# A TensorE-bound kernel: three reads of x in half-height tiles, and block products that put the second half's wide matmuls ahead of the first half's narrow ones

## The chip, the cores and the metric

One NeuronCore of a Trainium2 chip runs the kernel. The metric is device time in microseconds of one execution. Five engines work beside one another and wait for one another through semaphores: TensorE (PE; its weight loads are listed as PEld), VectorE (DVE), ScalarE (ACT), GpSimd (POOL) and SyncE (SP), which issues the DMAs.

## The reference

```python
def _attn_ref(x, state):                       # x 8,8,512,64   state 8,8,32,64
    scores = scale * np.matmul(x, state.transpose(0, 1, 3, 2))
    a = softmax(scores)                        # with 1e-9 added to the sum
    xread = np.matmul(a, state)
    scores2 = scale * np.matmul(state, x.transpose(0, 1, 3, 2))
    a2 = softmax(scores2)
    sread = np.matmul(a2, x)
    return np.concatenate([xread, sread], axis=2)

def reference(...):                            # 8*544 rows of 512
    x = attn_out.transpose(0, 2, 1, 3).reshape(B * S, H * D)
    g = softplus(x @ w_in)                     # 512 x 2048
    return g @ w_out                           # 2048 x 512
```

All is float32. "softmax" stands here for subtracting the maximum, exp, and dividing by the sum plus 1e-9.

## The kernel before, in words

The batches 0 to 7 each have 512 rows of x; the 32 state rows of all eight batches form a ninth block of 256 rows, called batch 8. Every kind of work is a generator, and every generator has a letter. The string PLAN (L40) is 1758 letters long; the loop at L977 takes it letter by letter and runs the next step of that generator. All instructions are kept in that order on their engine, so PLAN is the order of each engine's queue. For steps that several engines can do, ENG (L58) holds one letter a step: D for DVE, A for ACT, P for POOL. On-chip buffers are named rooms (L107), handed out first in, first out: eight PSUM banks (tiles named b), and in SBUF the classes s (12), d (17), g (8) and v (4).

The steps that matter here, by their letters:

- v (v_product) and Q (scores) call heads (L347): eight float32 matmuls of 64 rows by 32 columns of the array, in eight places of it, 512 columns each. The trace shows each as two matmuls.
- R (s_read, L541) multiplies the turned softmax a2T with x, one batch a step: for two values e, four chunks c and four column places q one float32 matmul of 128 rows by 32 columns with 64 columns moving, so 32 a step, 64 in the trace. The four chunks add up in one PSUM bank. r (s_scale, L557) multiplies the bank by the reciprocal sums on DVE and gives it back.
- t and y are transposes on TensorE, g (gemm1) is the first layer in groups of six 512-column matmuls, s is softplus on ACT.
- M (form_product, L868) is the second layer for batches 1 to 8. It is a block product with seven products in place of eight (the "forms" 1 to 7); each form of a team (a batch alone, the last team batches 8 and 7 together) is summed over two halves c = 0, 1. For each half, first come the "high" matmuls of 512 columns, then the "low" ones of 256 columns: 8 and 8 for a single batch, 12 and 12 for the last team. Then the half's operands are given back: Ahi and Alo (the split left operand) and Bt, the half's slab of weights, 1 MB in a g room. There are 49 forms, so 98 halves, in the order of UNITS2 (L796); the last half takes three M steps.
- J (slab_load, L800) fetches the slab of the next half from HBM into a g room. F, H and L (form_sum, form_hi, form_lo) prepare the left operand; k (chain) adds a finished product from its bank to the running sums; q (fold) and P (fold_store) finish and store them.

The functions that the change touches, with what calls them:

Of the kernel before, what the change touches and what calls it, by code (L numbers as in the profile page):

```python
# [15 lines left out]
ALU = mybir.AluOpType  # L16
# [3 lines left out]
P = 128  # L20
B, H, S, NS, D = 8, 8, 512, 32, 64
# [7 lines left out]
FAST = 1  # L29
F1, F2 = 4, 2  # L30
PIN = True


TURNS = [(0, 0, 16), (1, 0, 16)]
# [3 lines left out]
FORMS = (1, 2, 6, 5, 7, 3, 4)  # L38
# [8 lines left out]
    "q98MMtytvuhzHkkuLHlFFLZLhvRMMJJPJJMMHl9kHkhHLHhkLgMMlkirqkLqLklkkPTJJPPJJPJJXXvQvgse1fhshhlq1ell2qh3qggggsssfs"  # L47
    "4ggMgggsH2l53LgMg4ssssssgggssHs5Fk6ki7LFHFFHLFHFLtytMMMMkLH6uzkuLZqkHvvRJJJJPTMMhhLlHH7hlHh8q98FLLllkkrMMJJJTJ"
    "XPLFqHLqkk9HLMMgggMMsHsskkqkkkLkJPPJJPTJJXPvQv1khhql2qlee13ggggssshsHfhf42llLgggMgggsHFqL35sss4ssgggMsssH56F6k"
    "LFHkLFH7MMttyF8HqFLu7L9kuzHkLFMJPJPJJMMMJJPPJPPRvHZkkHFqLiLkHh8vMMkLlrHhHhHqLlLlkkH9LLqMJXPTJPPJJJJMgMggMssshk"  # L50
    "kHkklkkvvQge1hfsgggshsshH2Lll3h1l2leLFgggg4sssfsggggssssgMMM3FHFqsH4F5FqqLH5Lqk6LTPPJJJPMtytMMJJXJHFFHkLiuk7kH"
    "HHHzL6HLqLZkukLMMkFMvvRJJPh8hH7kLqlq9LrqLh8MMMJTJPXJJJPPXJPl9kHkhkkklgMMskklkvQvgghqHl1ehe2sfhfLlh13lqgggssss4"
    "Lq253qgggwiMyPssgHs45MgJzlsgFPLstkuJgkxsgssgtgsMH6sqL7H86PuMFZRLvvkrFJkhlvhlPvhhFFJHFLhlh97MHLlHHMHLMwFkMkHJJ8"
    "hLJJJlPq9MHgLkxsgkgMFsslPwgHgLJqPkLghkMqMgxkHsskgPkskgLJgJgsllqsPLMHLHyzMqZsPwssMkgggqLggskg&P&wsxsxMgkqwkx%%s"
    "wgswx&xqP&%s%s&g%w&wP%wJsxxgwJxxw&x%&%sF&gFw&wx%&%qxg%wHx&s&Lg%H%&sL%&&%s%sHLHLMFHMHFPFJFHHkJFLFLFLLFJkHMLMFJk"
    "JHLHFkkJMHHLHkLqMHkPLHkFLLJLJHMHLqLJHFkMHPFqkLJLHHkHPFLHMMLJkLMHLHkkkkLJMLqMkPkkHHqPqkqLkqLqPPqMPMkPqMPkqkPP"
)
ENG = {  # L58
    '&': "DDAADDADDDDADADA",
    '3': "PPDDDPPDPDDPDDDP",  # L60
    '6': "PPDPPPPDDPDDDPPP",
    '8': "PPDPAPDPDPPDAADPDD",
    '9': "DPDPDDDPPDPDDPDDPP",
    'B': "DAAADDAA",
    'D': "PDPAAADA",
    'E': "DDDPDPPD",
    'F': "DPDDDDDDPDPDPDDPDDPDPDDPDDPDPPDPPDPDPDDDPDPPDPPDDPDDDDPDDDDDDPDD",
    'H': "PAAAAPAAAADPAADAPAAAAAAPADPPAAPDDPPDAAPAADDAPDAADADDPAADAAAPAPAPAAPADAAAPAPAAAAPADADAADAAAAAAAAPAAAAPAAADAAAAPAA",
    'L': "DDDDDDDDPDPDPPPDDDDPPDDDPDPPPDPDDDPDDPPPPPDDPDDDPDDPDPDDDPDDDPDDDPDDDDPDPDPDDPPDPPPPPPDDDDDDDDDDPDPDPDDDPDDDDPDD",
    'U': "PPDDDPDP",  # L70
    'W': "AAADAPAD",
    'Y': "DDDPPPDD",
    'b': "AAAAADDDDD",
    'h': "AAAADADDDDDDDADAADADDDAADDAAADADAADDAADADAAAADAAAAADADADADADDAAAAAAA",
    'k': "AADDDDDDDDDDDDDDAADDDDDDDDDDDDDDAADDDDDDDDDDDDDDAADDDDDDDDDDDDDDDDDDDDDDDDDDDDDDAADDDDDDDDDDDDDDAADDDDDDDDDDDDDDDDDDDDDD",
    'm': "DAADAADAAAPADP",
    'n': "DDDPDDDPPDPDDD",
    'o': "AAAD",
    'q': "PPDPDPDDPDPDDPDPPPDDDDPPPPPPPDDPDDPPDDDPPPDDPDDDDPPPDPDPDDDD",
    'u': "DAADDAADDADADDDD",  # L80
    'w': "PADDADAAAAAAAAAA",
    'x': "DDPPPPDPDDDDDPDP",
    'z': "DDADAADA",
}


# [48 lines left out]
def attention_then_softplus_mlp(ctx: ExitStack, tc, xn, xt, zq, zp, stk, w_in, w_out, out):  # L135
    nc = Ordered(tc) if PIN else tc.nc
    TABLE = {AF.Softplus: "softplus", AF.Exp: "natural_log_exp_and_others", AF.Prelu: "natural_log_exp_and_others"}
# [14 lines left out]
    banks = Rooms(ps, "b", 8, [P, 512])  # L152
# [33 lines left out]
    xT, x, win, wraw = {}, {}, {}, {}  # L186
# [80 lines left out]
    up, low = {}, {}  # L267
# [122 lines left out]
    sc, T, e2, a2, pr, sr, aT = {}, {}, {}, {}, {}, {}, {}  # L390
# [21 lines left out]
    def rs(b, e):  # L412
        return few[b][:, 66 + e:67 + e]
# [118 lines left out]
    a2T = {}  # L532
# [7 lines left out]

    def s_read():  # L541
        for b in range(B):
            pr[b] = banks.take()
            for e in range(2):
                for c in range(4):
                    for q in range(4):
                        h = 2 * q + e
                        nc.tensor.matmul(pr[b][32 * q:32 * q + 32, D * e:D * e + D],
                                         a2T[b, e][:, P * c + 32 * q:P * c + 32 * q + 32],
                                         x[b, h // 4][:, c, D * (h % 4):D * (h % 4) + D], start=(c == 0), stop=(c == 3),  # L550
                                         tile_position=(0, 32 * q))
                a2T[b, e].done()
            x[b, 0].done()
            x[b, 1].done()
            yield

    def s_scale():  # L557
        for b in range(B):
            sr[b] = r1.take()
            nc.vector.tensor_tensor(sr[b].t.rearrange("p (e d) -> p e d", e=2), pr[b][:, 0:P].rearrange("p (e d) -> p e d", e=2),  # L560
                                    few[b][:, 66:68].unsqueeze(2).broadcast_to([P, 2, D]), ALU.mult)
            pr[b].done()
            few[b].done()
            yield

# [300 lines left out]
    prod = {}  # L866

    def form_product():  # L868
        for team, f, c in UNITS2:
            w = Bt[team[0], f, c]  # L870
            pairs = [(b, p) for b in team for p in range(1 if b == B else 2)]
            if c == 0:
                for k in pairs:
                    prod[k, f] = banks.take(uses=READS[f])
            def high(k, b, p):
# [7 lines left out]
            def low(k, b, p):  # L883
                nc.tensor.matmul(prod[(b, p), f][:, 0:256], Alo[b, f, c][:, k, P * p:P * p + P], w[:, k, 0],
                                 start=False, stop=(c == 1 and k == 3))

            if (team, f, c) == UNITS2[-1]:
                for n, pair in enumerate(pairs):
                    for of in (high, low):
                        for k in range(4):  # L890
                            of(k, *pair)
                    if n < 2:
                        yield
            else:
                for k in range(4):
                    for pair in pairs:
                        high(k, *pair)
# [50 lines left out]
    def fold_store():  # L948
# [90 lines left out]
```

## Time and profile before

| | us |
|---|---|
| median of 3 runs | 614.88 (614.83 to 615.35) |
| the profiled execution | 614.1 |
| its span, first to last instruction | 612.3 |
| PE busy | 597.5 (98%) |
| DVE, ACT, POOL busy | 477.1, 306.9, 303.9 |

The profile is of one execution on the one core. Busy time of PE is modelled at its ends and overlaps from one matmul to the next, so what a matmul costs is read from the distance of one start to the next and not from its duration. All operations bear line 100, a helper that records them, so rows are told apart by tiles and shapes.

### The profile page before, as it was taken

The numbers are of one execution on the slowest core, as the hardware profiler recorded it, in microseconds if no ns is written. First come the engines' busy times: TensorE is split into PE (matmuls) and PEld (weight loads), VectorE is DVE, ScalarE is ACT, GpSimd is POOL, SyncE is SP. The second block draws the span as 40 slices with busy tenths as digits, with TensorE's granted clock in tenths as the row PEclk, the third lists the DMA queues.
The fourth block names the chain that finished last, engine by engine and source line by source line (L and its number), as shares of the span: only waits on it lengthen the run. The fifth ranks groups of instructions, "written<-read, shape, count | busy, mean of one in ns | idle before, by whom it ended". The sixth has DMA issues, their size and how long they took to land.

```text
span 612.3 us, 10423 instructions
## 1 busy us (share of the span) xinstructions
PE 597.5 (98%) x4048; PEld 485.0 (79%) x4048; DVE 477.1 (78%) x644; ACT 306.9 (50%) x445; POOL 303.9 (50%) x190
## 2 busy tenths in 40 slices
PE   3999999999999999999999999999999999999997
PEld 1568677888788888878788787888787888888886
DVE  4999998799636896798479966699747944389996
ACT  4999767962526218631283318802675232274321
POOL 2422637517563761777276532672085955251561
PEclk9999999999999999999999999999999999999999
DMA  8999959999637888089917992699543851166572
GB/s 310 408 391 364 351 198 343 365 403 414 247 140 276 310 324 336 1 318 394 341 65 258 344 316 123 208 390 411 206 152 147 337 203 70 29 243 233 210 300 77
DMA packets 50415, 161.62 MB, mean 264 GB/s; under 512 B 4288, under 2 KB 29376, under 8 KB 37824
## 3 DMA queue, kind: packets, MB, share of 16 engines
q1 hardware_dynamic: 50368, 160.97, 70.5%
q8 instruction: 32, 0.52, 0.3%
q14 instruction: 15, 0.12, 0.1%
HBM read 137.36 MB, written 23.59 MB: 263 GB/s over the span
## 4 chain that ended last, share of the span: by engine, by line
PE 97%; DVE 1%; ACT 1%; DMA 1%; issue 0%; POOL 0%; SPq 0%
PE b L100 97%; ACT s L100 1%; DMA ST<-in_zp_dram 1%; DVE v L100 0%; DVE s L100 0%; POOL s L100 0%; SPq L100 0%; DVE W L100 0%; ACT ST L100 0%
## 5 line engine op out<-in xcount | busy, mean ns | idle before, releaser
L100 PE MATMUL b<-g,d 128*128 128x256 f32 (+1 forms) x1576 | 290.3, 337 | 0.0
L100 PEld LDWEIGHTS b<-g,d 128*128 128x128 f32 x1576 | 246.6, 190 | 36.1 <-issue 1.7
L100 PE MATMUL b<-d,d 128*128 128x512 f32 x744 | 177.2, 392 | 0.0
L100 PEld LDWEIGHTS b<-d,d 128*128 128x128 f32 x744 | 137.8, 188 | 32.3 <-issue 3.0
L100 ACT ACTIVATE g<-b 128x512 f32<-128x512 f32 x112 | 63.6, 600 | 98.7 <-PE b L100 98.3
L100 POOL TENSOR_TENSOR d<-g,d 128x1024 fp32r<-128x1024 f32 x31 | 78.6, 2538 | 53.0 <-ACT d L100 26.6
L100 DVE TENSOR_TENSOR s<-s,b 128x512 f32<-128x512 f32 (+1 forms) x105 | 68.7, 675 | 40.3 <-PE b L100 32.6
L100 DVE TENSOR_TENSOR d<-g,d 128x1024 fp32r<-128x1024 f32 x53 | 80.0, 1516 | 1.7 <-ACT d L100 1.5
L100 PE MATMUL b<-g,s 128*128 128x512 f32 (+1 forms) x280 | 71.4, 372 | 0.0
L100 ACT CAST d<-g 128x1024 fp32r<-128x1024 f32 x50 | 51.7, 1051 | 29.7 <-POOL g L100 15.8
L100 ACT ACT_TABLE_LOAD x48 | 61.6, 1283 | 1.5 <-PEq L1020 0.7
L100 PEld LDWEIGHTS b<-g,s 128*128 128x128 f32 x280 | 50.2, 188 | 12.0 <-issue 2.2
L100 ACT CAST d<-b 128x512 fp32r<-128x512 f32 x35 | 20.1, 586 | 59.3 <-PE b L100 59.3
L100 DVE TENSOR_TENSOR d<-b,d 128x512 fp32r<-128x512 f32 x62 | 41.4, 681 | 9.3 <-ACT d L100 9.0
L100 POOL TENSOR_SCALAR d<-g 128x1024 fp32r<-128x1024 f32 x20 | 29.5, 1476 | 36.2 <-DVE g L100 26.5
L100 POOL TENSOR_TENSOR s<-s,v 128x512 f32<-128x512 f32 x17 | 21.0, 1237 | 44.5 <-DVE v L100 43.9
L100 POOL TENSOR_TENSOR s<-s 128x256 f32<-128x256 f32 x29 | 29.9, 1032 | 21.1 <-DVE s L100 21.1
L100 POOL TENSOR_TENSOR d<-d,d 128x256 f32<-128x256 f32 (+2 forms) x17 | 28.3, 1664 | 18.6 <-DVE d L100 8.5
L100 PE MATMUL b<-W,ST 64*32 64x512 f32 (+2 forms) x544 | 32.6, 574 | 4.1 <-DVE W L100 4.1
L100 DVE TENSOR_REDUCE v<-s 128x16 f32<-128x512 f32 x32 | 21.6, 680 | 18.6 <-ACT s L100 18.5
L100 POOL TENSOR_TENSOR g<-g,g 128x1024 f32<-128x1024 f32 x11 | 29.4, 2671 | 11.2 <-DVE d L100 6.3
L100 ACT COPY s<-b 128x512 f32<-128x512 f32 (+2 forms) x32 | 15.2, 501 | 29.1 <-PE b L100 25.1
(82 smaller groups left out, 626.9 us busy)
## 6 DMA issues: line engine op xcount, KB each, us to landing
g<-slabs SPq DMA_DIRECT2D x98, 1024.0 KB, 6.6
d<-in_xt_dram SPq DMA_DIRECT2D x16, 512.0 KB, 7.4
g<-in_w_out_dram SPq DMA_DIRECT2D x8, 1024.0 KB, 12.5
d<-in_xn_dram SPq DMA_DIRECT2D x16, 512.0 KB, 7.6
slabs<-d SPq DMA_DIRECT2D x16, 512.0 KB, 6.9
out_dram<-s SPq DMA_DIRECT2D x56, 128.0 KB, 5.3
g<-in_w_in_dram SPq DMA_DIRECT2D x6, 1024.0 KB, 13.0
slabs<-g SPq DMA_DIRECT2D x24, 256.0 KB, 7.1
```

Of the source, the lines that this page charges most:

```text
L100: return lambda *a, **k: self.tc.keep_in_program_order(f(*a, **k))
```

## The change

Three things are changed.

SPLIT gives each batch a number of row halves for its read. For batches 4, 5 and 6 it is 2: each matmul of 128 rows becomes two of 64 rows, in the upper and the lower half of the array, which add up in two PSUM banks; s_scale then scales the first and adds the second with one scalar_tensor_tensor on DVE for each e. The other batches read as before.

JOIN has one letter for each of the 49 forms. At 20 of them it is J: the step of the half c = 0 issues its high matmuls alone and ends; the step of c = 1 issues its own high matmuls, then the low ones of half 0, gives the operands of half 0 back, then the low ones of half 1, and gives those back. The 29 others run as before. The forms with J are five of batch 2, six of batch 3, four of batch 4, four of batch 5 and one (form 7) of the last team.

PLAN is the same in its first 702 letters and in its last 53 and in another order between, with the same count of every letter. ENG changes for some of the steps.

```diff
+SPLIT = (1, 1, 1, 1, 2, 2, 2, 1)
+JOIN = ("--------JJJJJ-JJJJJJ-J-JJ--J-JJ-JJ------------J--")
...
     def s_read():
         for b in range(B):
-            pr[b] = banks.take()
+            halves = SPLIT[b]
+            pr[b] = [banks.take() for _ in range(halves)]
+            n = P // halves
             for e in range(2):
                 for c in range(4):
                     for q in range(4):
-                        h = 2 * q + e
-                        nc.tensor.matmul(pr[b][32 * q:32 * q + 32, D * e:D * e + D],
-                                         a2T[b, e][:, P * c + 32 * q:P * c + 32 * q + 32],
-                                         x[b, h // 4][:, c, D * (h % 4):D * (h % 4) + D], start=(c == 0), stop=(c == 3),
-                                         tile_position=(0, 32 * q))
+                        for o in range(halves):
+                            h, r = 2 * q + e, slice(n * o, n * o + n)
+                            nc.tensor.matmul(pr[b][o][32 * q:32 * q + 32, D * e:D * e + D],
+                                             a2T[b, e][r, P * c + 32 * q:P * c + 32 * q + 32],
+                                             x[b, h // 4][r, c, D * (h % 4):D * (h % 4) + D], start=(c == 0), stop=(c == 3),
+                                             tile_position=(n * o, 32 * q))
...
+            if SPLIT[b] == 2:
+                for e in range(2):
+                    t = sr[b][:, D * e:D * e + D]
+                    nc.vector.scalar_tensor_tensor(t, pr[b][1][:, D * e:D * e + D], rs(b, e), t, ALU.mult, ALU.add)
...
     def form_product():
+        held = []
         for team, f, c in UNITS2:
...
+            for k in range(4):
+                for pair in pairs:
+                    high(k, *pair)
+            held.append(c)
+            if c == 0 and JOIN[len(FORMS) * TEAMS.index(team) + FORMS.index(f)] == "J":
+                yield
+                continue
+            for d in held:
                 for pair in pairs:
                     for k in range(4):
-                        low(k, *pair)
-            for b in team:
-                Ahi[b, f, c].done()
-                Alo[b, f, c].done()
-            w.done()
+                        low(k, *pair, d)
+                finished(d)
+            held.clear()
             yield
```

The order of the TensorE steps around the reads of batches 4 to 7 goes from `vvR`, `Rvv`, `vvR`, `Rvvvv` to `Rvv`, `vvR`, `Rvv`, `Rvvvv` (each with M steps on both sides).

## Rows read from the trace of the kernel before

**Rows 1.** The page: span, busy time of the engine with most, granted clock by slice.
```profile
span 612.3 us, 10423 instructions
...
PE 597.5 (98%) x4048; PEld 485.0 (79%) x4048; DVE 477.1 (78%) x644; ACT 306.9 (50%) x445; POOL 303.9 (50%) x190
...
PEclk9999999999999999999999999999999999999999
```

**Rows 2.** The chain that ended last, shares by engine.
```profile
PE 97%; DVE 1%; ACT 1%; DMA 1%; issue 0%; POOL 0%; SPq 0%
```

**Rows 3.** The same chain in order of time: start us, us, what.
```profile
18.40 590.13 PE b L100 x3956
```

**Rows 4.** Waits of PE, longest and shortest of four: waiter, awaited, us in total, times, longest.
```profile
PE b L100 <- DMA ST<-in_zp_dram: 5.1, 1, 5.1
...
PE b L100 <- ACT s L100: 0.7, 1, 0.7
```

**Rows 5.** Timeline of PE: start, us, instructions; a read beside two or four heads calls.
```profile
342.15 1.10 PE L100 MATMUL b<-d,s 128*32 128x64 f32 x64
343.18 1.95 PE L100 MATMUL b<-W,ST 64*32 64x512 f32 x32
345.06 3.30 PE L100 MATMUL b<-g,d 128*128 128x512 f32 x17
...
413.07 1.95 PE L100 MATMUL b<-W,ST 64*32 64x512 f32 x32
414.95 1.10 PE L100 MATMUL b<-d,s 128*32 128x64 f32 x64
415.98 8.29 PE L100 MATMUL b<-g,d 128*128 128x512 f32 x45
...
468.15 3.66 PE L100 MATMUL b<-W,ST 64*32 64x512 f32 x64
471.75 2.11 PE L100 MATMUL b<-g,d 128*128 128x512 f32 x8
```

**Rows 6.** Busy time in the stretch of the first weight loads.
```profile
5.04:5.19 0.15, 0.09 (x8) 0.12 (x16) 0.00 (x0) 0.00 (x0) 0.00 (x0) 1.00 0.90 294
```

**Rows 7.** Timeline of PE, narrow stretches: where blocks of high and low matmuls start.
```profile
188.50 0.39 PE L100 MATMUL b<-g,d 128*128 128x512 f32 x1
190.31 0.52 PE L100 MATMUL b<-g,d 128*128 128x256 f32 x3
191.26 0.63 PE L100 MATMUL b<-g,d 128*128 128x512 f32 x2
193.10 0.52 PE L100 MATMUL b<-g,d 128*128 128x256 f32 x3
194.06 0.63 PE L100 MATMUL b<-g,d 128*128 128x512 f32 x2
```

**Rows 8.** A slab load's issue, the unit it feeds, landing times in 190 to 204.
```profile
191.46 0.33 SPq L100 DMA_DIRECT2D g<-slabs  x1
...
199.64 0.63 PE L100 MATMUL b<-g,d 128*128 128x512 f32 x2
...
DMA to landing us min/median/max: 4.7/4.8/5.0
```

**Rows 9.** Groups of DVE by shape: busy us, mean ns.
```profile
L100 DVE TENSOR_TENSOR d<-g,d 128x1024 fp32r<-128x1024 f32 x53 | 80.0, 1516 | 1.7 <-ACT d L100 1.5
L100 DVE TENSOR_TENSOR g<-g,g 128x1024 f32<-128x1024 f32 x17 | 23.0, 1356 | 0.4 <-ACT g L100 0.4
...
L100 DVE TENSOR_TENSOR v<-b,v 128x128 f32<-128x128 f32 x8 | 2.3, 282 | 2.6 <-PE b L100 2.5
```

**Rows 10.** Busy time of PE, PEld, DVE, ACT, POOL before and in the last team.
```profile
480.00:545.00 65.00, 65.00 (x345) 55.95 (x344) 35.76 (x58) 21.08 (x43) 33.38 (x20) 1.00 0.42 159
545.00:612.30 67.30, 63.51 (x373) 56.16 (x371) 57.30 (x73) 22.66 (x36) 27.91 (x18) 1.00 0.59 213
```

More of the change, by code (lines that the diff above doesn't have):

```diff
@@ L46 @@
     "gggsLkssss4vvMMgh5qkhlkHhdhsqLLqlllgMgggggMsssssFq67HkLJJJPJPPPXggggMssssHF8LHsHFM6LF7FHFLLkkHMMJJJPJHHkkqqkLL"
[L47 to L55, printed above, removed]
@@ L56 @@
-    "JHLHFkkJMHHLHkLqMHkPLHkFLLJLJHMHLqLJHFkMHPFqkLJLHHkHPFLHMMLJkLMHLHkkkkLJMLqMkPkkHHqPqkqLkqLqPPqMPMkPqMPkqkPP"
+    "q98MMtytvuhzHkkuLHlFFLZLhvRMMJJPJJMMHl9kHkLLgihhPqJJMHkkkgsTlMPkTHQrvklXsPvJhkXlh1LghXl23gJls1Jeqsg2ghsqs4fqg3"
+    "sg5MyFHsg4LgeLglf56gssgggssPgsMssFsFFHHqJkFLMPMHLtFH7HkJuJLtkMMH6J8LuRivHrkkvLqhhJMkPMJFHJlM9TL7PHklkJLFLzMZ8L"
+    "kPMH9hkMgHMkqsLkJqhLllgkgMTkHkQk1svHsvgseghglgsq2f3hgJlX41hsLLg2sHL3gle5sP4hlgs5sJqggqgFg6sssgs678sPsFMJMMkFfq"
+    "HHPHJkFLFMJt7qqLkykMLtHF9HJ8uJLMkPLHuJXPPMMvHh9JkzhJvkRkLLZJFlMMlhgPJkHgJHqLJsFMirLhHgJHlkMskLLPkMPMkTTskkqQHl"
@@ new lines @@
+    "vkJe1vgshgeX2hlhqshXgPlJgJgsTLsHqggss1l32fLlHgsgggsqgMsssLFPsHgFMs4LHMJFyfFPJt5LFiutqzJMMuk3HHFkq4J5HFPLM6LJM7"
+    "HLJqqMkRkJL6HkvHkHqk8Lrkv7hhqHllZMM9FhL8kJJkP9LlhMMgLHJksMkLMkvJPkkvHhlQkyhLlPgg1sz2gHPJsswggqhlhJ1LsJsPPegPXs"
+    "H23Zqefqf4LFMglMlgg53sgqisgsgPskg4sgP5skss6gq6JHMLtxtsFHquwPMHFkuFRvPJ7rLvFLh8hkvHlvlJMJFhlHhHLMlkhL9J7H8l9MMg"
+    "gkshFskHghsJkPqLMJFgsgsLgHMlLlJhJMsgHgqgssLkHsLPgkgMlksLJqPkygMgkkxPgqMwxsPkzHwqgsZHsksgg&%JwxxgwxLs&P%gqswxw&"
+    "wPM%&xLsJ&x%gw%&s&%&M%kwsx%gswxwxF&FgwxHqk&xg%&&w%Jsx&%&%wsx%gJH&%%LLJs&J%sFFFHHLMHFHHLFPFLFMLLMkFHFHLFMkJHHkk"
@@ L57 @@
+    "JqHHLLMLkHLPHMkLFLJLHMJqLJkkHHFLLJqMPHLqHkkJPFLPkHHFLJHHMMLJkLMHLHkkkkLJMLqMkPkkHHqPqkqLkqLqPPqMPMkPqMPkqkPP"
 )
 ENG = {
[L59 to L63, printed above, removed]
+    '&': "AAAADAAAAADDADDA",
+    '3': "PPDDDPPDPDPDDDPP",
+    '6': "PPDPPPPDDDPDDPDD",
+    '8': "PPDPAPDPDPPADAAPAA",
+    '9': "DPDPDDDPPDDPPPDDPD",
     'B': "DAAADDAA",
@@ L66 @@
     'E': "DDDPDPPD",
-    'F': "DPDDDDDDPDPDPDDPDDPDPDDPDDPDPPDPPDPDPDDDPDPPDPPDDPDDDDPDDDDDDPDD",
-    'H': "PAAAAPAAAADPAADAPAAAAAAPADPPAAPDDPPDAAPAADDAPDAADADDPAADAAAPAPAPAAPADAAAPAPAAAAPADADAADAAAAAAAAPAAAAPAAADAAAAPAA",
-    'L': "DDDDDDDDPDPDPPPDDDDPPDDDPDPPPDPDDDPDDPPPPPDDPDDDPDDPDPDDDPDDDPDDDPDDDDPDPDPDDPPDPPPPPPDDDDDDDDDDPDPDPDDDPDDDDPDD",
+    'F': "DPDDDDDDPDPDPDDPDDPDPPPPDDDPDDDDDDPDPDPDDDPPDPPPDDDDDDDDDDDDPDDD",
+    'H': "PAAAAPAAAADPAADAPAAAAAAPADPDAAAPAADAAAAPDADAAPDDDPDPDPPAPDDDADAPAAPDDAPDPAAAPPPDDPDPPAAAPAAAAAAADDAPAADDAAPAAPAA",
+    'L': "DDDDDDDDPDPDPPPDDDDPPDDDDPPPPDPDDDPPDPPPPDPPDDDPDPPDPDPDPDDDDPDPPDDDDPDDPPDDPDPDDDDDPDDDDDDDDDPDPDDDPDDPPDDDDPDD",
     'U': "PPDDDPDP",
@@ L73 @@
     'b': "AAAAADDDDD",
-    'h': "AAAADADDDDDDDADAADADDDAADDAAADADAADDAADADAAAADAAAAADADADADADDAAAAAAA",
-    'k': "AADDDDDDDDDDDDDDAADDDDDDDDDDDDDDAADDDDDDDDDDDDDDAADDDDDDDDDDDDDDDDDDDDDDDDDDDDDDAADDDDDDDDDDDDDDAADDDDDDDDDDDDDDDDDDDDDD",
+    'h': "AAAADADDDDDDDADAADADDDAADDAAADADDDDDDDAADDDAAAAAAAAAADAAAAAAAADAAADD",
+    'k': "AADDDDDDDDDDDDDDAADDDDDDDDDDDDDDDDDDDDDDDDDDDDDDAADDDDDDDDDDDDDDDADDDDDDDDDDDDDDDDDDDDDDDDDDDDDDAAADDDDDDDDDDDDDDDDDDDDD",
     'm': "DAADAADAAAPADP",
@@ L78 @@
     'o': "AAAD",
[L79 to L83, printed above, removed]
+    'q': "PPDPDPDDPPPDDDPDPDDPPPDPPDPDPDDPPDDPDDDDPDDPDDDDDDPPDPDPDDDD",
+    'u': "DAADDAADAADDAAAA",
+    'w': "DAPDAADADDAPAAAP",
+    'x': "DPDDDPDPDPPDDDDP",
+    'z': "DDADADDA",
 }
@@ L559, in s_scale @@
             sr[b] = r1.take()
-            nc.vector.tensor_tensor(sr[b].t.rearrange("p (e d) -> p e d", e=2), pr[b][:, 0:P].rearrange("p (e d) -> p e d", e=2),
+            nc.vector.tensor_tensor(sr[b].t.rearrange("p (e d) -> p e d", e=2),
+                                    pr[b][0][:, 0:P].rearrange("p (e d) -> p e d", e=2),
                                     few[b][:, 66:68].unsqueeze(2).broadcast_to([P, 2, D]), ALU.mult)
-            pr[b].done()
+            if SPLIT[b] == 2:
+                for e in range(2):
+                    t = sr[b][:, D * e:D * e + D]
+                    nc.vector.scalar_tensor_tensor(t, pr[b][1][:, D * e:D * e + D], rs(b, e), t, ALU.mult, ALU.add)
+            for t in pr[b]:
+                t.done()
             few[b].done()
@@ L874, in form_product @@
                     prod[k, f] = banks.take(uses=READS[f])
+            last_unit = (team, f, c) == UNITS2[-1]
             def high(k, b, p):
@@ L881, in high, with low, finished @@
                                      start=(c == 0 and k == 0 and y in (0, slice(0, 2))), stop=False)
[L883 to L887, printed above, removed]
+            def low(k, b, p, d):
+                nc.tensor.matmul(prod[(b, p), f][:, 0:256], Alo[b, f, d][:, k, P * p:P * p + P], Bt[team[0], f, d][:, k, 0],
+                                 start=False, stop=(d == 1 and k == 3))
+            def finished(d):
+                for b in team:
+                    Ahi[b, f, d].done()
+                    Alo[b, f, d].done()
+                Bt[team[0], f, d].done()
+            if last_unit:
                 for n, pair in enumerate(pairs):
-                    for of in (high, low):
-                        for k in range(4):
-                            of(k, *pair)
+                    for k in range(4):
+                        high(k, *pair)
+                    for k in range(4):
+                        low(k, *pair, 1)
                     if n < 2:
                         yield
[L894 to L897, printed above, removed]
+                finished(1)
+                yield
+                continue
+            for k in range(4):
+                for pair in pairs:
+                    high(k, *pair)
+            held.append(c)
+            if c == 0 and JOIN[len(FORMS) * TEAMS.index(team) + FORMS.index(f)] == "J":
+                yield
+                continue
+            for d in held:
                 for pair in pairs:
                     for k in range(4):
-                        low(k, *pair)
-            for b in team:
-                Ahi[b, f, c].done()
-                Alo[b, f, c].done()
-            w.done()
+                        low(k, *pair, d)
+                finished(d)
+            held.clear()
             yield
```

## The prediction

> **What bounds the kernel now.** [...] Then the waits of PE. There are four in all, none over 5.1 us and 11 us together [rows 4], and all lie in the first 18.4 us, where the chain passes through loads, DVE and ACT; from there on it is PE alone for 590.1 us, up to 608.5 [rows 3]. So the time of this kernel is the sum of the starts of its matmuls, and a change can do only two things: alter that sum, or bring in a wait where there is none. A wait that is taken away is worth nothing here.
>
> The change keeps every count of steps, its first 702 letters and its last 53, so the start, where the four waits are, and the tail behind the last matmul (612.3 less 608.5 us) stay. The profiled execution took 614.1 us for a span of 612.3; the median of the runs is 614.88, so 0.8 above it. I make the sum as a difference and apply it to the median.
>
> **The reads, batches 4 to 6.** A read takes 1.03 us from its first start to the next step's, whether a heads call follows (342.15 to 343.18) or a 512-column matmul (414.95 to 415.98) [rows 5]. Two heads calls with a change of tile shape behind them take 1.88 us (343.18 to 345.06), four take 3.60 (468.15 to 471.75). So a heads call costs 0.86 us, and one change of tile shape 1.88 - 2 x 0.86 = 0.16 us. Taken off the read, that leaves 0.87 us for 64 matmuls, 16 rounds over four places at 54 ns. A split read has 128 matmuls in 16 rounds over eight places. A round in heads, 512 columns in place of 64, takes 0.86 / 2 = 430 ns, eight times 54: so the columns set a round's length, and with 64 columns it stays 54 ns if eight starts fit in it. The split read then costs the same 0.87 us, and it has the shape of the heads calls beside it, in all three cases (`Rvv`, `vvR`, `Rvv`): one change of shape of 0.16 us is gone from each. Three times: 0.48 us less.
>
> Bounds: do eight starts of a matmul and its weight load fit in 54 ns? At the start of the kernel, where the queue had just been held by a wait, 8 matmuls and 16 weight loads of this shape start within 0.15 us [rows 6], about 6 ns for each instruction or 100 ns for eight pairs; but the window is wider than the burst. From above: if pairs come no faster than in the read of before, 0.87 / 64 = 13.6 ns each, a split read takes 1.74 us, three cost 2.6 us more, and with the saved changes of shape it is 2.1 us to the bad. I take the value with no extra time, since heads, the same shape in the same order of places, keeps its rounds at the length that the columns give, and keep the range -0.5 to +2.1 us.
>
> [...]
>
> On DVE the split adds six scalar_tensor_tensor of 128 by 64 from PSUM. The nearest row is 282 ns for twice that size [rows 9]: 1.7 us at most, off the path while DVE is idle for 22% of the span. The second bank is held from the read to s_scale; what that costs is one bank less for a few us, at three places, zero if the next product's bank is free by then, and up to a DVE step of 0.7 us if not.
>
> **The joined products.** Each high and low matmul is still run. What changes is how often 256 columns follow 512. Eight highs behind gemm1's 512-column matmuls take 188.50 to 190.31, 1.81 us; behind a block of lows they take 191.26 to 193.10, 1.84. Eight lows take 0.95 and 0.96 [rows 7]. So high matmuls behind lows cost 0.03 us a block more, and lows behind highs perhaps 0.01 less than later lows. A joined form replaces two such changes by one and saves about 0.02 us; 20 forms: 0.4 us less. With starts read to 0.01 us the bounds are 0 and -0.8 us. None of the 20 has a change of tile shape between its two halves' highs, so none loses the gain to that.
>
> What a join delays: the slab of half 0 comes free behind 16 highs and 8 lows in place of 8 and 8, so 1.8 us later, and with it Ahi and Alo of that half. Slab loads run on a ring here: the load issued at 191.46, right behind the unit that ended, feeds the unit that starts at 199.64, 8.2 us later, and lands 4.8 us after its issue [rows 8]. 3.4 us are to spare, and a join takes 1.8 of them where the ring is that tight. So a join alone brings no wait at a landing of 4.8 us and one of up to 1.6 us at a landing of 8, if other loads are ahead of it. In front of the J on SP stand stores that wait for DVE; a store that is late holds the loads behind it.
>
> **The new order.** The number of stretches with small tiles on PE stays 8 in the changed part, that of transposes goes from 7 to 8, with the same transposes; I take 0, within 0.1 us. The change of engines moves work: by the counts in ENG, DVE gets 8 more H casts, 6 more q, 3 more F and fewer of others, some 14 us net beside the 1.7, ACT and POOL lose 13 and 6. At 493 of 612 us DVE is not the bound on average. The place to look at is the end: of the extra DVE work some 10 us lie before the last team's products, where DVE is busy 35.8 of 65 us, and 1 us in them, where it is busy 57.3 of the 63.5 us that PE has left [rows 10]. In the first stretch it fits; I take no wait.
>
> **Sum.** -0.5 (reads) - 0.4 (joins) + 0 = -0.9 us, from which I take back 0.1 for a bank or an operand that comes late somewhere: 614.88 - 0.8 = **614.1 us**, which is 0.13%. A measurement of this kernel can tell about 0.2%, 1.2 us, from no change.
>
> **Rivals.**
> 1. *A new wait, slower.* For it: PE had no wait, so every other order can only add some, and DVE works without a pause in the last team. If the 10 us of DVE work ahead of the last team can't start early, because its inputs come from PE, they run into a stretch with 6.2 us of DVE idle (63.5 - 57.3): 3.8 us of wait. Or two or three joined pairs wait 1 us each for a slab. Against: the first stretch has 29 us of DVE idle, and a slab has 1.6 us to spare after a join. Time: 614.1 + 2 to 4, so 616.1 to 618. It decides from 2.0 us of wait on, where the gain is eaten and 0.2% passed.
> 2. *The split reads are longer.* It decides where eight pairs don't start in 54 ns; at the read's present pace of 13.6 ns a pair: 614.88 + 2.1 - 0.4 = 616.6 us, slower.
> 3. *Nothing is left of it*: the saved changes of shape return as idle of the array between the last head and the first read, or the joined lows cost what the change of width did. 614.9 us.
> 4. *More than I read*: the joins at their bound of 0.8, the reads at 0.5: 613.6 us, just over 0.2% faster.
>
> **How the numbers follow.** Forecast 45%, rival 3 20%, rival 1 17%, rival 2 6%, rival 4 12%. The forecast and rival 3 lie within 0.2%; of rival 1 a few hundredths are waits that only eat the gain. Faster 0.13, same 0.67, slower 0.20. The range reaches down to 613.3, a little under rival 4, and up to 616.6, which takes in rival 2 and the smaller waits of rival 1.
>
> **What the changed profile would show.** PE's matmuls go from 4048 to 4240, 192 more, with the reads of batches 4 to 6 as 128 of 64 by 32. A stretch of two heads calls and a read takes 2.77 us in place of 2.91. If the read's part there is over 1.2 us, rival 2 holds. A joined form (16 highs, then 16 lows) takes 5.56 us in place of 5.58. The waits of PE are the same four; a fifth one behind 220 us means rival 1, and its releaser says which: DVE d or s (operands or banks) or a DMA of slabs. Last matmul: 607.7 in place of 608.5 us. I am wrong if PE's sum moves by over 1.2 us without a wait.

## The result, and the profile after

The changed kernel takes 618.22 us (617.27 to 619.52, six runs) against 614.83 (614.49 to 615.35, six runs) for the kernel before: a ratio of 1.0051, 95% interval 1.0041 to 1.0062. It is slower by 3.4 us, outside the forecast's range. The profiled execution took 619.52 us for a span of 616.7, 2.8 us more than the span; before it was 1.8 more.

The page of the changed kernel, where [rows 1] stood:

```profile
span 616.7 us, 10804 instructions
...
PE 599.4 (97%) x4240; PEld 486.8 (79%) x4240; DVE 492.3 (80%) x662; ACT 286.6 (46%) x427; POOL 302.3 (49%) x188
...
PEclk9999999999999999999999999999999999999999
```

The 192 added matmuls are there, the clock is at its full level throughout, and DVE has grown by 15 us. TensorE's busy time has grown by only 1.9 us, and the span by 4.4. So the page says that most of the loss is not work. The waits of PE, where [rows 4] stood (waiter, awaited, us in total, times, longest), say what it is:

```profile
PE b L102 <- DMA ST<-in_zp_dram: 5.0, 1, 5.0
PE b L102 <- DVE W L102: 4.1, 1, 4.1
PE b L102 <- DMA d<-in_xt_dram: 2.5, 1, 2.5
PE b L102 <- issue: 1.4, 2, 0.8
PE b L102 <- DMA g<-slabs: 0.4, 1, 0.4
PE b L102 <- ACT s L102: 0.4, 1, 0.4
```

Two rows are new: a wait for a slab, and two stretches put down to "issue", which means that TensorE waited for no semaphore that the profile shows. The end of the chain in order of time, where before one piece of 590.13 us stood [rows 3], says where:

```profile
279.38 7.95 DMA g<-slabs
287.34 0.14 issue
287.47 60.60 PE b L102 x443
348.08 0.76 issue
348.83 66.57 PE b L102 x475
415.40 0.60 issue
416.00 197.22 PE b L102 x1248
613.22 0.02 issue
613.25 0.42 DVE s L102
```

Both "issue" stretches lie in split reads. The timeline of PE around the read of batch 5 (start us, us, instructions, in brackets the idle time before them), where [rows 5] showed the same region before:

```profile
344.96 1.95 PE L102 MATMUL b<-W,ST 64*32 64x512 f32 x32
346.70 1.37 PE L102 MATMUL b<-d,s 64*32 64x64 f32 x113
348.83 0.34 PE L102 MATMUL b<-d,s 64*32 64x64 f32 x15 [0.76 <-issue]
349.11 0.50 PE L102 MATMUL b<-g,d 128*128 128x512 f32 x1
```

After 113 of its 128 matmuls the read stops, and the last 15 come 0.76 us later. Two heads calls and a read take 4.14 us (344.96 to 349.11) in place of 2.91 (342.15 to 345.06 in [rows 5]). In batch 6 it is 3.94, in batch 4 3.57 us.

**The account.** From the first 128-column matmul behind batch 3's read, where PLAN begins to differ, to the start of the last matmul, the kernel before takes 399.02 us and the changed one 402.31: 3.29 more. The three regions with split reads give 2.93 of it ((3.57 + 4.14 + 3.94) - 3 x 2.91). The next two terms are counted by starts against experiment 1, which runs the same matmuls but for the split. Two matmuls behind joined forms of batch 3 come late, at 284.98 us by 0.30 and at 287.47 by 0.65, each some 0.15 us behind the landing of a slab; the list of waits shows the second alone. The joined products with the new order give -0.39 in experiment 1, and -0.65 without a delay of 0.26 at 339.10 us that experiment 1 has and this execution has not. 2.93 + 0.95 - 0.65 is 3.23; 0.06 is left. The rest is outside: from the last matmul to the end of the execution it was 5.9 us and is 6.5 (below, experiments 1 and 12). The first part, up to that point, is the same program in all kernels here but experiments 9 and 12, save for three joined forms of batch 2 from 196 to 204 us, worth some 0.04 us. It ended at 209.21 us before and at 210.62 in this profiled execution; over the other traces it ended between 210.02 and 211.27, so the profiled execution of before was the early one, and I put none of this 1.4 us down to the change.

### The profile page after: what moved, and what is told of

The parts are those of the page before. It is cut to its first block, busy times and chain, and to the rows that moved or that the text cites. A ratio compares the mean times of both kernels' runs of the same rounds, so it can differ in the third digit from the quotient of the medians.

```text
span 616.7 us, 10804 instructions
## 1 busy us (share of the span) xinstructions
PE 599.4 (97%) x4240; PEld 486.8 (79%) x4240; DVE 492.3 (80%) x662; ACT 286.6 (46%) x427; POOL 302.3 (49%) x188
## 4 chain that ended last, share of the span: by engine, by line
PE 95%; DMA 2%; DVE 1%; ACT 1%; issue 0%; SPq 0%; ACTq 0%
PE b L102 95%; DMA g<-slabs 1%; DMA d<-in_xt_dram 1%; ACT s L102 1%; DVE v L102 0%; DVE s L102 0%; SPq L102 0%; DVE W L102 0%; ACTq L102 0%
## 5 line engine op out<-in xcount | busy, mean ns | idle before, releaser
L102 POOL TENSOR_TENSOR d<-g,d 128x1024 fp32r<-128x1024 f32 x30 | 76.7, 2558 | 77.9 <-ACT d L102 34.6
L102 DVE TENSOR_TENSOR d<-g,d 128x1024 fp32r<-128x1024 f32 x54 | 85.6, 1590 | 6.2 <-POOL d L102 4.6
L102 ACT CAST d<-g 128x1024 fp32r<-128x1024 f32 x41 | 42.1, 1049 | 23.9 <-POOL g L102 8.1
L102 POOL TENSOR_TENSOR g<-g,g 128x1024 f32<-128x1024 f32 x12 | 31.9, 2657 | 19.1 <-DVE d L102 11.0
L102 ACT CAST d<-b 128x512 fp32r<-128x512 f32 x33 | 18.6, 588 | 47.1 <-PE b L102 47.1
L102 POOL TENSOR_TENSOR d<-d,d 128x1024 fp32r<-128x1024 f32 (+2 forms) x18 | 31.4, 1745 | 14.4 <-DVE d L102 7.8
L102 ACT COPY s<-b 128x512 f32<-128x512 f32 (+2 forms) x39 | 18.4, 489 | 41.0 <-PE b L102 36.7
L102 POOL TENSOR_TENSOR s<-s 128x256 f32<-128x256 f32 x25 | 26.0, 1040 | 19.9 <-DVE s L102 19.9
L102 DVE TENSOR_TENSOR d<-g 128x1024 f32<-128x1024 f32 x12 | 17.6, 1467 | 11.3 <-ACT g L102 10.2
```

The source lines that it names most:

```text
L102: return lambda *a, **k: self.tc.keep_in_program_order(f(*a, **k))
```

## The experiments

**1. No split, joins and order as changed.**

```diff
-SPLIT = (1, 1, 1, 1, 2, 2, 2, 1)
+SPLIT = (1, 1, 1, 1, 1, 1, 1, 1)
```

> The changed kernel with every read in the old shape; joins and order kept. [...] The slab wait near 285 us (0.8 us) stays. Theory B (the new order and the joins cost it, by late slabs and operands): the time stays within 1 us of 618.2.

Measured: 614.64 us against 614.96, ratio 0.9997 (0.9988 to 1.0006). The whole loss is gone with the split. (Experiments 3 and 4 reckon from 615.3 us for this run: 618.2 less 2.9, the three regions of 3.57, 4.14 and 3.94 us at 2.91 each.) The chain is one piece of PE again to its end:

```profile
339.10 269.85 PE b L102 x1795
608.95 0.02 issue
608.97 0.42 DVE s L102
```

The main part is 398.63 us, 0.39 under the kernel before, and the list of waits has none for a slab. Yet the median gains 0.3 where the span gains 0.8 (612.4 against 613.2): outside the span it loses 0.55, 2.33 us in place of 1.77 (all medians over the runs), which is taken up in experiment 12.

**2. Only batches 5 and 6 split, and 3. only batch 6.** SPLIT is (1, 1, 1, 1, 1, 2, 2, 1) and (1, 1, 1, 1, 1, 1, 2, 1).

> The changed kernel with batch 4 read in the old shape, 5 and 6 split. The idle stretches of 0.97 and 0.81 us inside the reads of batches 5 and 6 come at PE instructions 5057 and 6081, 1024 apart, both 193 past a multiple of 256; a block of 256 instructions is fetched while the one before runs. Without batch 4's 64 extra pairs the reads of 5 and 6 begin 128 instructions earlier in their block. Theory A1 (a block boundary meets the end of a read that began near the boundary before it): both idle stretches are gone, the regions of batches 5 and 6 take 3.1 to 3.3 us, the time is some 618.2 - 1.8 - 0.7 = 615.7. Theory A2 (the idle belongs to these reads whatever the count before them, for instance to loads that run beside them): both stay, 617.5.

> The changed kernel with batch 6 alone split, so its read begins 256 instructions earlier, at the same place of a block as in the changed kernel. Theory A1: the idle stretch of about 0.8 us is back in batch 6's read, region 3.9 us, and the time is about e1's + 1.0, some 616.3, above or near e2 although it has half the split reads. Theory A2: the same idle. If only the number of dense matmuls over the whole run mattered: no idle, region 3.1.

Measured: 616.02, ratio 1.0018 (1.0009 to 1.0028), and 616.40, ratio 1.0025 (1.0014 to 1.0036). No region has an idle stretch in either; all three split regions take 3.20 us. The read of batch 5 in experiment 2 shows what a split read costs when nothing else happens:

```profile
343.44 1.95 PE L102 MATMUL b<-W,ST 64*32 64x512 f32 x32
345.18 1.52 PE L102 MATMUL b<-d,s 64*32 64x64 f32 x128
346.64 0.50 PE L102 MATMUL b<-g,d 128*128 128x512 f32 x1
```

3.20 us against 2.91: the split costs 0.29 us a read, with one change of tile shape already saved. Windows of 0.22 us through that read show its pace (us of the window, busy, instructions; a matmul lasts about 0.22 us here, so each window counts those under way and those that start, half and half in a steady stretch):

```profile
345.18:345.40 0.22, 0.22 (x28) 1.00 0.95 261
345.40:345.62 0.22, 0.22 (x39) 1.00 0.53 223
345.62:345.84 0.22, 0.22 (x44) 1.00 1.43 335
345.84:346.06 0.22, 0.22 (x47) 1.00 0.81 186
```

46 or so, half of which start there, are 23 in 0.22 us, 9.6 ns a matmul. The starts themselves say a little more: 1.27 us (batch 6) and 1.31 us (batch 5) from the first of 128 to the last, 10 ns on average. The same windows over a full-height read of the kernel before hold 31 or 32, 16 starts, 13.7 ns. The first 16 to 32 starts of a split read are for the most part 6 to 7 ns apart, then 5 and 11 in turn, in stretches 16 to 17. The first pace is the one that the prediction needed for 54 ns a round; it doesn't last. What sets the one pace or the other is not shown.

Experiment 2's main part is 1.04 us over experiment 1's. Its two split reads are 0.58 of that; the rest is short delays near 339, 402 and 418 us.

Experiment 3 should have kept its idle stretch if the place of the code alone decided. It had none, and still was 1.8 us above experiment 1. Experiment 11 repeats it.

**4. No split, and the join of one form of batch 3 taken back.** JOIN[16] is "-" in place of "J".

> The changed kernel with every read in the old shape and one join taken out (batch 3, form 6: halves 32 and 33), whose slabs come free late and feed halves 36 and 37, for which PE waited near 285 us. Theory A (late slab by the join): the slab of half 32 comes free 1.8 us earlier, the wait of 0.8 us is gone, the time is 0.8 below e1, 614.5. Rival (the loads land late by other traffic, not by the join): the wait stays, the time is e1's.

Measured: 614.98, ratio 1.0000 (0.9992 to 1.0009). It told nothing, since experiment 1 had no slab wait for it to remove.

**5. The split reads' matmuls among those of a heads call.**

```diff
+    pending = []
     def heads(out_e, b, rhs):
...
                                  tile_position=(64 * e, 32 * q))
+                for _ in range(8):
+                    if pending:
+                        f, t = pending.pop(0)
+                        f(*t)
...
-                            nc.tensor.matmul(...)
+                pending.append((one, t))
```

> The 128 matmuls of each split read (batches 4, 5, 6) are issued eight at a time behind each matmul of one heads call, in place of all in one row; for batch 5 the read moves one heads call earlier. Nothing is left out. Theory A (TensorE runs out of instructions: the fetched ones are used up in a row of 128 short matmuls, faster than the next come): the heads matmuls give the supply time, so no idle stretch within the read, and the region of two heads calls and a read takes 2.75 to 2.85 us, below the 2.91 of the unsplit read; total as in the run without any split, 614.1 to 615.0 us. Theory B (the array itself needs 9.4 ns for each matmul of a 64x32 tile, wherever it stands): the region stays at 3.2 us as in the run that splits 5 and 6, total 615.5 to 616.5.

Measured: 625.38, ratio 1.0169 (1.0155 to 1.0182). Both theories fell: the regions take 5.7 to 7.0 us. The start of batch 6's region:

```profile
417.69 0.61 PE L102 MATMUL b<-W,ST 64*32 64x512 f32 x1
417.71 0.34 PE L102 MATMUL b<-d,s 64*32 64x64 f32 x14
418.15 0.93 PE L102 MATMUL b<-W,ST 64*32 64x512 f32 x2
418.58 0.51 PE L102 MATMUL b<-d,s 64*32 64x64 f32 x16
```

Fourteen read matmuls start in 0.12 us beside the heads matmul; then nothing starts for 0.32 us, up to the second half of the same heads call's matmul. Such stops, of 0.16 to 0.36 us, come all through the three regions; batch 4's, the one of 7.0 us, also holds a wait of 0.4 us for a bank. What holds the matmuls there is not shown. Long and short matmuls mixed in this way take 5.7 to 7.0 us a region where 3.20 do for them in a row (experiments 2 and 3), and the two theories are not told apart here.

**6. Each split read in two steps with a heads call between.**

```diff
                 a2T[b, e].done()
+                if halves == 2 and e == 0:
+                    yield
```

PLAN gets a second R for batches 4, 5 and 6, so that their order is `RvRv`, for batch 5 with the chain step that stood between ahead of it.

> The split reads of batches 4, 5, 6 are issued in two steps of 64 matmuls (e = 0, then e = 1), with a heads call between (for batch 5 the read moves by half a step). Nothing is left out. Theory A: each half starts with a filled supply, so its first matmuls come at 6.7 ns; region 2.9 to 3.0 us, and where a fetch of instructions starts just ahead of the read, as it did in batches 5 and 6, an idle stretch of at most 0.5 us is left, since about 0.9 us of heads lie between. Total 614.5 to 615.7. Theory B: region 3.2 us in each, no idle stretch; 615.5 to 616.5.

Measured: 618.79, ratio 1.0056 (1.0044 to 1.0069). Theory A's forecast of 2.9 to 3.0 us was wrong: 4.47, 4.55 and 3.37. The heads call between does not bring the first pace back: in batch 6, without any idle stretch, the second half takes 0.86 us from first to last start against 0.64 for the first. Batch 4's region holds a wait of 0.4 us for a bank. In batch 5 the idle stretch came, as expected of a fetch near the read, but at 1.09 us in place of 0.5:

```profile
346.99 0.77 PE L103 MATMUL b<-d,s 64*32 64x64 f32 x49
348.85 0.34 PE L103 MATMUL b<-d,s 64*32 64x64 f32 x15 [1.09 <-issue]
```

**7. The changed kernel again.**

> The changed kernel as it is, a second time. Theory A: again 617.7 to 618.7 us, ratio 1.005; the two idle stretches of TensorE of 0.8 to 1.0 us within the reads of batches 5 and 6 come back at the same places, since the blocks of instructions lie where they lay. Rival: the stretches were a chance of that execution; regions 3.2 to 3.6 us and the excess sits in the first 20 us.

Measured: 617.91, ratio 1.0041 (1.0027 to 1.0054). Regions of 3.58, 3.98 and 3.34 us, 2.17 over the unsplit ones: the idle stretch of batch 5 is there again, that of batch 6 only as a gap of 0.2. The slab wait came again (0.7 us, at 286.9 us), the main part is 401.46, 2.44 over before. So theory A holds in place, and the size of the stretches varies with the execution.

**8. The joins alone, in the old order.** Before's PLAN and ENG, with the new form_product and JOIN.

> The kernel before with its own order and engines, and only the 20 joined forms. Theory A (joins save 0.02 us each): 614.4 us, 0.4 below the kernel before, span about 0.4 us shorter, no wait of TensorE behind 20 us. Rival: the old order has no room for the later release of the slabs, one to three waits of 0.5 to 1.6 us for a slab; 615.4 to 617.

Measured: 614.95, ratio 0.9998 (0.9990 to 1.0007), no wait behind 20 us, the same 1.8 us outside the span, main part 398.79 us. By these traces, one of each, the joins give 0.23 us; with the new order it is 0.39. The times of the runs can't tell it.

**9. The code shifted.** The first round of batch 3's read is issued four times more: 128 instructions of TensorE ahead of the split reads.

```diff
-                for c in range(4):
+                for c, spare in ([(0, True)] * 4 if b == 3 else []) + [(c, False) for c in range(4)]:
...
-... start=(c == 0), stop=(c == 3),
+... start=(c == 0), stop=(spare or c == 3),
```

> The changed kernel, with the first four-column round of the read of batch 3 issued four times more (its results are overwritten by the fifth, so the output is the same): 64 matmuls and 64 weight loads, 128 instructions of TensorE, more ahead of the split reads. Theory A (an idle stretch comes where a 16 KB fetch of 256 TensorE instructions starts just ahead of a split read): with 128 instructions more the fetches start in the middle between reads, as in the run that splits 5 and 6 alone; regions of batches 5 and 6 are 3.20 us each with no idle stretch of over 0.1 us, that of batch 4 3.2 to 3.6. Batch 3's region is 2.91 + 0.88 = 3.79 us. The main part from batch 3's read to the last matmul is 0.8 to 1.8 us below that of the changed kernel; total 616.8 to 618.0. Rival (the stretches belong to batches 5 and 6, to what is loaded or computed beside them): they stay at 0.8 us and more, total 618.5 to 619.3.

Measured: 621.34, ratio 1.0106 (1.0093 to 1.0120). The total is above both forecasts, and from batch 3's read to the last matmul it is 405.65 us against 403.34 in the changed kernel, 2.3 more where theory A said 0.8 to 1.8 less. But the two regions in question are what theory A said, 3.20 us each without a gap (here batch 5):

```profile
347.97 1.95 PE L102 MATMUL b<-W,ST 64*32 64x512 f32 x32
349.71 1.53 PE L102 MATMUL b<-d,s 64*32 64x64 f32 x128
351.17 0.50 PE L102 MATMUL b<-g,d 128*128 128x512 f32 x1
```

The stretches have moved to the other two: batch 3's read, which now has 128 matmuls, and the heads calls behind batch 4's.

```profile
209.12 1.87 PE L102 MATMUL b<-d,s 128*32 128x64 f32 x116
212.49 0.42 PE L102 MATMUL b<-d,s 128*32 128x64 f32 x12 [1.50 <-issue]
...
276.33 1.08 PE L102 MATMUL b<-W,ST 64*32 64x512 f32 x13 [0.99 <-issue]
```

What goes with TensorE's release is in the DMA queues. One queue of the kind "instruction", q8, has packets of 16 KB: 33 to the 8480 matmuls and weight loads of the changed kernel, 32 to the 8096 of before, one for about 256 on average. By these counts I take them for TensorE's instructions. In the changed kernel one starts 0.22 us ahead of batch 5's read, at 346.49 us, and takes 1.0 us; this is the queue's row (packets, MB, share) for 346.4 to 346.6 us:

```profile
q8 instruction: 1, 0.02, 31.5%
```

In experiment 9 the one before batch 5's read starts at 341.10, 8.6 us ahead of it. Every idle stretch within a region from 0.2 us up that no wait for a bank explains, those of experiment 5 apart, ends at nearly the same distance from the start of such a packet:

| stretch | packet starts | matmuls go on | us between |
|---|---|---|---|
| changed kernel, batch 5 | 346.49 | 348.83 | 2.34 |
| changed kernel, batch 6 | 413.56 | 416.00 | 2.44 |
| again (7), batch 5 | 345.59 | 348.13 | 2.54 |
| again (7), batch 6 | 412.44 | 414.68 | 2.24 |
| two steps (6), batch 5 | 346.41 | 348.85 | 2.43 |
| shifted (9), batch 3 | 210.20 | 212.49 | 2.29 |
| shifted (9), batch 4 | 274.15 | 276.33 | 2.18 |
| batch 6 again (11) | 410.97 | 413.44 | 2.47 |

So TensorE went on some 2.2 to 2.5 us after a packet had started. A split read uses up 256 instructions in some 1.3 us. In the five split reads in one row with a packet 0.2 to 0.9 us ahead of them TensorE stops; where the packet starts 1.9 us ahead (experiment 3) or 8 us and more (2 and 9), it doesn't. The unsplit read has 128 instructions: in experiment 1 a packet starts 0.52 us ahead of batch 6's read, and nothing is lost.

How many matmuls and weight loads were left when the packet started differs: 218 to 238 in those five, 107 in experiment 6, 77 and 5 in experiment 9. What the eight have in common shows when one counts from the start of the packet before: 506 to 545 had started when TensorE stopped, about two packets' worth. It is 547 at a stop of 0.17 us in experiment 10, and 498 and 497 at two stops of 0.2 and 0.4 us outside the regions (experiment 2 at 418.04 us, experiment 9 at 422.67), both 2.2 us behind the start of a packet. At every other packet of these traces it was below 495 at 2.15 us behind the packet's start, but for two that reached 506 and 510 and went on (batch 6 in 10 and in 6). The packets don't come evenly, 54 to 418 matmuls and weight loads apart in the changed kernel and 44 to 530 in experiment 9. What makes one start late is not shown.

**10. As many matmuls, at full height.** Each product of the split reads is made twice at 128 rows, once for each bank, so these three reads come out doubled.

```diff
-... a2T[b, e][r, P * c + 32 * q:P * c + 32 * q + 32],
+... a2T[b, e][:, P * c + 32 * q:P * c + 32 * q + 32],
...
-... tile_position=(n * o, 32 * q))
+... tile_position=(0, 32 * q))
```

> The changed kernel, with the split reads' matmuls at full height again (128 rows by 32 columns) but as many: each product is made twice, once for each bank, so the reads of batches 4, 5 and 6 come out doubled. 128 matmuls a read as in the changed kernel, of the tile shape of before. Theory A: the array takes 13.7 ns a pair, slower than instructions come, so a read is 1.76 us; region 2.91 + 0.88 = 3.79 us for batch 4, and 3.8 to 4.5 for batches 5 and 6, where a fetch starts just ahead of the read and 256 instructions are still used up in less than the 2.4 us that it needs (0.3 to 0.7 us idle). Rival: 13.7 ns a pair is slow enough, no idle stretch, 3.79 us in all three; then it is the pace of the half-height tiles and not the number of instructions that empties the supply. Total 618.0 to 620.0 under either.

Measured: 619.47, ratio 1.0073 (1.0060 to 1.0086). Regions of 4.16, 4.05 and 3.87 us, with packets 0.65 and 0.74 us ahead of batches 5 and 6:

```profile
344.63 1.95 PE L102 MATMUL b<-W,ST 64*32 64x512 f32 x32
346.51 2.24 PE L102 MATMUL b<-d,s 128*32 128x64 f32 x128
348.68 0.50 PE L102 MATMUL b<-g,d 128*128 128x512 f32 x1
```

Batch 6's read has no idle stretch: it takes 1.85 us from first to last start, as batch 4's does, which has no packet near it, so some 3.87 us is what 128 matmuls of this height cost. Batch 5's has a stop of 0.17 us by starts, 2.44 us behind its packet. That lies between theory A's 0.3 to 0.7 us and the rival's nothing, nearer to the rival: at this pace 256 instructions take 1.8 us, which with the 0.65 us ahead of them nearly come to the 2.44, where half-height tiles leave up to 0.9. The number of instructions and the pace both count: 128 at full height lost nothing behind a packet 0.52 us ahead (experiment 1), 256 lost nothing or 0.17 us, 256 at half height up to 0.94. Batch 4's extra 0.29 us is a wait for a bank like the one described below.

**11. Only batch 6 split, again.**

> The kernel that splits batch 6 alone, a second time: its time was 1.8 us over that without splits, of which its trace showed 0.3 in the read and some 1 us in the first 10 us. Theory A (the rest was chance in the loads at the start): 615.0 to 615.6, first read of batch 3 at 209 us as in the others. Rival (a property of this program): again 616.2 to 616.8 with a start that is 1 us late.

Measured: 615.75 (614.65 to 617.25, 11 runs), ratio 1.0014 (1.0005 to 1.0023). This time the region is 3.89 us and has its idle stretch, and the start is 0.6 us earlier than in experiment 3:

```profile
411.54 1.37 PE L102 MATMUL b<-d,s 64*32 64x64 f32 x114
413.44 0.28 PE L102 MATMUL b<-d,s 64*32 64x64 f32 x7 [0.53 <-issue]
```

The packet started 0.57 us ahead of the read, in the other execution 1.88. So the same program has the stretch in one execution and not in another. Of experiment 3's 1.8 us over experiment 1, 1.1 are left in the second sample: 0.3 for the read and up to 0.7 for the stretch. The rest is not explained.

**12. No split, instruction counts as before.** Seven one-column copies more on ScalarE and nine on GpSimd.

```diff
             pr[b] = [banks.take() for _ in range(halves)]
+            if b < 7:
+                cast(spare[:, 0:1], ident[:, 0:1], "A")
+            for _ in range(2 if b == 7 else 1):
+                cast(spare[:, 1:2], ident[:, 0:1], "P")
```

> The kernel without splits (new order, 20 joins), with seven copies of one column more on ScalarE and nine on GpSimd, one or two at each read, so that these two engines have as many instructions as in the kernel before (577 and 328). Nothing is left out. Theory A (time outside the span, 2.3 us against 1.8 before, is a fetch of code at the very end that falls elsewhere as ScalarE's and GpSimd's instruction counts change): the 8 KB fetch 2.1 us behind the span's end is gone or earlier, 1.8 us outside the span, total 614.1 to 614.5. Rival: outside the span stays at 2.3 us, total 614.6 to 615.0.

Measured: 615.28, ratio 1.0004 (0.9995 to 1.0013); outside the span 1.79 us, as before. The other queue of the kind "instruction", q14, has packets of 8 KB (15 in the changed kernel's span, 0.12 MB); I take them for the other engines' code. These are its rows behind the end of the span: of experiment 12, within 0.5 us of the end; of experiment 1, 1.6 to 3.6 us behind it; of the changed kernel, 1.3 to 3.3 us behind it.

```profile
q14 instruction: 2, 0.02, 8.6%
```

```profile
q14 instruction: 1, 0.01, 1.2%
```

```profile
q14 instruction: 3, 0.02, 5.0%
```

In the kernel before and in experiment 8 there are two, within 0.3 us of the end, and 1.8 us lie outside the span. With the new order's counts one or two come 2.1 to 2.4 us behind the end and some 2.3 lie outside; in the changed kernel, with the three split reads' six instructions more on DVE, a further one comes at 1.6, the others at 2.5, and 2.75 lie outside. These are medians over the runs. Before, and in experiments 8 and 12, single executions lie from 1.7 to 1.9 us, those of the changed kernel from 2.2 to 2.8; experiment 7, the same program with the same three packets, has one of 3.4, so the packets don't explain all of it. Theory A holds for experiment 12's part outside the span. But the total didn't follow: with the packets early the span itself ends 0.4 us later behind the last matmul (4.22 us against 3.78), and this execution took 0.65 us more in its main part than experiment 1, 0.2 of it at a slab, at 339 us. From the last matmul to the end of the execution (up to the end of the span by the trace, behind it the median) it is 5.9 us before, 6.1 in experiment 1, 6.0 in 12, 6.5 in the changed kernel.

No kernel of these beats both. The best, experiment 1, is the kernel before within what can be told.

## Why the prediction was wrong, point by point

**What bounds the kernel.** Right, by [rows 1] and [rows 2] too, and it was the reason for the loss: with TensorE on the path from 18 us on, each idle stretch of it is the kernel's.

**The reads: the step that failed.** "The split read then costs the same 0.87 us": three times -0.16, -0.48 us in all. The three regions measured +2.93 us in the profiled execution and +2.17 in the second one. Its terms, from the undisturbed region of 3.20 us (experiments 2, 3 and 9):

- The pace: 0.29 us a read over before, 0.87 in all, where -0.48 was forecast. The saved change of shape came (-0.16), so the read itself takes 0.45 us more. "With 64 columns it stays 54 ns if eight starts fit in it": they fit for the first 16 to 32 matmuls and then not. I leaned on the heads calls and on the burst of [rows 6] for a steady rate; two heads calls have 32 matmuls in 1.7 us, and their pace says nothing of 128 in 1.3. Rival 2 named this and priced it at 2.1 us by the pace of full-height matmuls, 13.6 ns; it was about 10.
- The idle stretches: 0.94 and 0.74 us, in the second execution 0.78 and 0.14. No part of the prediction had them. Both ends of its range for the reads priced what the array needs, and none asked whether instructions come that fast; so the reads' +2.93 us lies above the end of +2.1.
- A bank, 0.38 us in batch 4. There the read comes ahead of two heads calls, and all but the first matmul of the second call start only when DVE has emptied the read's second bank:

```profile
271.26 2.33 PE L102 MATMUL b<-W,ST 64*32 64x512 f32 x28
273.52 0.50 PE L102 MATMUL b<-g,d 128*128 128x512 f32 x1
```

```profile
271.47 0.29 DVE L102 TENSOR_TENSOR v<-b,v 128x128 f32<-128x128 f32 x1 [0.24 <-PE b L102]
271.88 0.47 DVE L102 SCALAR_TENSOR_TENSOR v<-b,v,v 128x64 f32<-128x64 f32 x2
```

The 28 heads matmuls last 2.33 us where the same read in batch 6 has 31 in 1.92: of the second call one starts at 272.03 and the other 15 from 272.46 on, behind 272.35, the end of the second scalar_tensor_tensor. "Up to a DVE step of 0.7 us if not" had the mechanism and a fair size, and only its place in the sum (0.1 us for all such things) was too small.

**The joined products.** -0.4 forecast, -0.23 measured alone, -0.39 with the new order, whose own part was put at 0. Right within its bounds of 0 to -0.8, and the size of one was right: where nothing comes between, a joined form of experiments 1 and 8 takes 5.57 us from its first high matmul to the step behind its lows, two halves of before 5.59. Alone, the joins lose 0.11 of their gain in one stretch, 338 to 341 us.

**The new order.** DVE grew by 15.2 us, where 14 and 1.7 were forecast, and the one new wait of TensorE for DVE is the bank's. "DVE works without a pause in the last team" was misread: from 545 us to the end of the span before, DVE is idle for 9.8 us, some 6 of them ahead of the last matmul, as the prediction's own 6.2 says.

**The later release of the slabs.** "One of up to 1.6 us at a landing of 8": both profiles of the changed kernel have it, behind the joined forms of batch 3. The matmuls that wait for it and the loads of slabs from 262 to 290 us (least, median and longest time from issue to landing):

```profile
287.47 1.39 PE L102 MATMUL b<-g,d 128*128 128x512 f32 x5 [0.40 <-DMA g<-slabs]
```

```profile
DMA to landing us min/median/max: 6.2/7.8/10.9
```

The one waited for was issued at 279.38 and landed at 287.34, 8.0 us later, where [rows 8] had 4.8; counted by starts it costs 0.65 us, and the slab before it, issued at 278.42 and landed 6.4 us later, 0.30. So rival 1 came in, at less than half of its lowest price of 2 us. In experiment 1, with the same joins, order and loads, the landings of that stretch are 4.8 to 9.1 us and nothing waits; in the runs with batch 4 unsplit no execution waits at this place, though two do at 339. Whether the split of batch 4 causes it or only moves it into a slow moment of the DMA queue stays open.

**The tail.** "The tail behind the last matmul stay[s]": wrong by 0.6 us in the median. The extra time goes with 8 KB packets of q14 behind the end, and experiment 12 took back 0.54 us outside the span by instruction counts alone; that the packets cause it is not shown beyond this, and the 3.4 us of one execution of experiment 7 are more than they explain.

**The sum.** Of the two profiled executions' main parts, 3.29 and 2.44 us over before, and 0.64 for the tail, 3.1 to 3.9 us come together; the medians are 3.4 and 2.8 apart. What is left between them is less than the start of single executions varies (210.0 to 211.3 us at the same instruction).

Of the marks set for the changed profile, the count of matmuls came; so did the joined form within 0.01 us (5.57); the region of 2.77 us (2.75 by its own terms), the four waits and the last matmul at 607.7 (612.9) didn't. "If the read's part there is over 1.2 us, rival 2 holds" is what the clean regions show, at 1.27 us from first to last start. "I am wrong if PE's sum moves by over 1.2 us without a wait" came true as well: pace and idle stretches, 2.55 of the reads' 2.93 us, came without a wait for a semaphore.

## What to carry to other kernels

Before long matmuls are cut into more and shorter ones on an engine without slack, divide the time of the dense stretch by its instructions, weight loads included: a price from a burst of 32 (here 6 to 7 ns a start) is not one for a row of 128 (10 ns, experiment 2). Without a semaphore to wait for, TensorE stopped here where some 500 to 550 matmuls and weight loads had started since the start of one 16 KB packet and the next was not yet 2.2 us old. A split read starts 256 of them in some 1.3 us; where the point falls moves with instructions added ahead (experiment 9) and from one execution to the next (experiments 3 and 11). Such a stop is found in the trace by "issue" idle time and a packet of the instruction queue 2.2 to 2.5 us before it ends. Instructions on engines beside the path count too: with sixteen copies more on ScalarE and GpSimd the last 8 KB packet came within 0.5 us of the span's end in place of 2.1 behind it, and 1.79 us lay outside the span in place of 2.33 (experiment 12).

## What the runs showed of the hardware that I had not expected

- The queue q8 has a packet of 16 KB for about 256 matmuls and weight loads on average (33 to 8480), and TensorE went on 2.2 to 2.5 us after one had started (eight stretches). It stopped where 497 to 547 matmuls and weight loads had started since the start of the packet before.
- Matmuls of 64x32 with 64 columns start 6 to 7 ns apart in the first 16 to 32, 10 ns on average in a row of 128 (experiment 2); at 128x32 13.7 ns (the kernel before).
- A heads call between two half reads did not restore the first pace (experiment 6, batch 6: 0.64 us, then 0.86 for 64 matmuls, first to last start).
- Short matmuls put among long ones stopped for 0.16 to 0.36 us again and again (experiment 5); three regions that take 3.2 us without a stop became 5.7 to 7.0.
- The time outside the span went with 8 KB packets of q14 behind its end: in the median 1.8 us where the last comes 0.3 us behind it, 2.3 where at 2.1, 2.75 where at 2.5; one execution with the last at 2.5 has 3.4.
